# Opening of a fused Nyström attention and MoE kernel: p0 behind the values, identity products in waits, decode ahead of sums

## The chip, the core and the metric

The kernel runs on one core of a Trainium2 chip. Time is device time of one execution in microseconds (us), lower is better. The kernel before took 795.48 us, the median of three runs (795.26, 795.48 and 796.25). The core has five engines with their own instruction streams: PE (matrix products), DVE (vector), ACT (scalar functions, copies), POOL (general), and SP, which here only issues transfers to the DMA engines.

## The reference

Eight batches of attention over 576 positions and 8 heads of 64, with 32 landmarks and an iterated inverse, then one gated feed-forward network over all 4608 tokens:

```python
q_lm, k_lm = means of 18 consecutive rows of q, k      # 32 landmarks
A  = sm(q, k_lm); Bm = sm(q_lm, k_lm); C = sm(q_lm, k)  # softmax of scaled products
Z = Bm.T / (norm1(Bm) * norminf(Bm) + 1e-6)
for _ in range(6):
    Z = 2 * Z - Z @ Bm @ Z
x = (A @ Z @ C @ v) laid out as 4608 x 512
xn = x / sqrt(mean(x * x) + 1e-6) * rms_g
g = xn @ w_gate; val = xn @ w_val                       # 512 x 1536 each
out = (g * sigmoid(g) * val) @ w_out                    # 1536 x 512
```

Everything is float32.

## The kernel before

**Stages.** A batch's attention treats two groups of four heads. `sums` (DVE, line 599) makes the landmark sums of q and k. `Front` makes the scores of landmarks against all positions on PE (`sC`, `sA`), their maxima on DVE, and exponentials on ACT (`E`). `turn` transposes `E` on PE (`sE`, `sF`) and ACT copies it out (`ET`, `EL`). `values` multiplies it with v (PE, `pCV`), and ACT or DVE scales that into the right columns of `PV`. `newton_start` works on the small matrices `Bm` (DVE: `BT`, norms, `nden`). `bmm(BT, BT)` is the first product of the inverse (`p0`, shown as `p<-BT`), and `newton_first` scales it into the left columns of `PV` (DVE, line 1023). Then six `newton_step`s alternate a PE product of 8 pieces (`pn`) with a DVE update (line 1040). `newton_weights` makes the products `pW` and from them `W` and `WT`, and `second` makes the attention output in turned form and its RMS scale: products `pO`, squares on ACT, row sums `pss`, DVE transposes `sqT`, product `pms`, a chain of nine small DVE instructions (lines 1112 to 1126), and at the end the operand `an` as a high and a low part (ACT line 1142, DVE line 1146).

**Feed-forward.** Attention's last matrix is not applied to the tokens: `mix_weights` multiplies the gate and value weights of a pair of 128-column blocks with it (`pM`), and splits the result in `Mhi` and `Mlo` (for the first pair the low part is made by subtracting on PE with the matrix `minus`). `mlp` then walks pairs of blocks: products `psg` (gate) and `psv` (value) of 6 instructions each, silu on ACT (line 528), product with the value half on DVE (line 529), split into `h` (lines 533, 534), and after three pairs the output products `pso`. The weights arrive as raw bytes and are decoded by two ACT instructions (lines 194, 196) and one DVE instruction (line 204) for each block. Block f of the gate is called f-gate below, of the values f-value; pair n holds blocks 2n and 2n+1.

**What sets the order.** Products on PE keep the order in which the program writes them. In `opening()`, the attention of batch 0, all instructions of the other engines are pinned in written order too (`own=pin`). Afterwards `Mixer` weaves the attention of batch 1 (`steady`) into the products of chunk 0: the list `at` says behind which product slot of `mlp` each piece goes (54 for softening, 84, 91, ... for the six Newton steps, 126 for `pW`, `n_gv` = 144 is where the output products begin). On DVE and ACT a scheduler orders what the program leaves free.

**Holds and identity products.** `landed(x)` issues a tiny transfer of one number of x to a scratch tensor (`told`). SP issues transfers in order and holds at the `told` until x has landed, so later loads are held back as well. `spare(n)` and `idle(out, n)` issue n products of the identity with itself into an unused corner of PSUM (`psw<-ident`); nothing reads them. Each float32 product shows as two matmuls in the trace.

**Loads.** SP issues q and k of batch 0, v (512 and 64 KB for a group), then raw weight blocks (`fetch`, line 169, 510.5 KB each) and q and k of batch 1 (`load_qk`, line 584, two of 576 KB for a group). q and k of batch 1 reuse the buffers of batch 0, so their issue waits until PE has read those.

Of the kernel before, what the change touches and what calls it, by code (L numbers as in the profile page):

```python
# [20 lines left out]
P = 128  # L21
# [38 lines left out]
def nystrom_moe_kernel(  # L60
# [53 lines left out]
    def mm(*args, **kw):  # L114
        tc.keep_in_program_order(nc.tensor.matmul(*args, **kw))  # L115
# [155 lines left out]
    def until(chunk, n):  # L271
        while mix.at < (chunk, n):
            yield 0.0
# [299 lines left out]
    with tc.tile_pool(name="ap", bufs=1, side="right") as ap, tc.tile_pool(  # L573
# [6 lines left out]
        def load_qk(b, g):  # L580
            t = qp.tile([P, 2, 2, S], F32, name=f"qk{b}{g}", tag="qk", bufs=2)
            loaded[b, g] = [t[:, 0], t[:, 1]]
            for z in range(2):
                nc.sync.dma_start(loaded[b, g][z], (q, k)[z][b, g])
# [157 lines left out]
        def spare(n):  # L742
            idle(pg.tile([P, 512], F32, name="psw", tag="pg")[:, :P], n)

        def turn(b, g, more=0, own=free):
            E = state[b]["E"][g]
            sE = pa.tile([P, 4, P], F32, name="sE", tag="pa")
            for ch in range(4):
                tp(sE[:, ch], E[:, ch * P : (ch + 1) * P], ident)
            room = pa.tile([P, 2, P], F32, name="sF", tag="pa")  # L750
            sF = room[: 2 * M, 0]
            tp(sF, E[:, 4 * P :], ident)
            idle(room[:, 1], more)
            ET = ap.tile([P, 4, P], F32, name="ET", tag="ET", bufs=2)
            EL = ap.tile([2 * M, P], F32, name="EL", tag="EL", bufs=2)
            own(nc.scalar.copy(ET, sE))
            last = own(nc.scalar.copy(EL, sF))
            if (b, g) == (1, 1):
                early.after = last.ins
            state[b]["ET", g] = ET, EL  # L760
# [21 lines left out]
            else:  # L782
                pin(nc.scalar.mul(to, pCV, by))

        told = dram.tile([1, 2], F32, name="told", tag="told")
        told_at = itertools.count()

        def landed(x):
            n = next(told_at)
            nc.sync.dma_start(told[:, n : n + 1], x)  # L790

        def opening():
            b, own = 0, pin
            for g in range(2):
                sums(b, g, None if g else made.ins, own=own)
            one, two = fronts = [Front(b, g, own) for g in range(2)]
            early.fetch()
            landed(loaded[b, 0, "v"][0][:1, 0, 0, :1])
            for _ in range(3):
                early.fetch()  # L800
            load_qk(1, 0)
            landed(early.raws[1, "v"][0][:1, 0, 0, :1].bitcast(F32))
            load_qk(1, 1)
            for _ in range(4, NF1 + RAWS):
                early.fetch()
            for part in fronts:
                part.tops()
            for part in fronts:
                part.exps()
            one.turned()  # L810
            one.totals()
            two.turned(es=(0,))
            two.totals()
            turn(b, 0, 3, own)
            turn(b, 1, 0, own)
            start = newton_start(b, own)
            BT, den = next(start)
            p0 = bmm(BT, BT, M, "p0")
            for g in range(2):
                values(b, g, 1 - g)  # L820
                load_v(1, g)
            for _ in range(2):
                early.fetch()
            newton_first(b, p0, den, own)
            two.turned(es=(1,))
            lower(b, 0, own=own)
            newton_step(b, 0, own)
            spare(2)
            lower(b, 1, own=own)
            newton_step(b, 1, own)  # L830
            spare(2)
            ends = [early.begin(own) for _ in range(2)]
            expose(b, 0, own)
            expose(b, 1, own)
            ends.extend(early.begin(own) for _ in range(2))
            sums(1, 0, zs=(0,), own=own)
            newton_step(b, 2, own)
            spare(2)
            next(start, None)
            shares(b, 0, own)  # L840
            newton_step(b, 3, own)
            spare(2)
            shares(b, 1, own)
            newton_step(b, 4, own)
            spare(2)
            back(b, 0, own)
            newton_step(b, 5, own)
            spare(2)
            back(b, 1, own)
            newton_weights(b, own)  # L850
            spare(1)
            parts = second(b, own)
            next(parts)
            sums(1, 0, zs=(1,), own=own)
            next(parts)
            ends.extend(early.begin(own) for _ in range(2))
            for _ in range(4):
                ends.pop(0)()
            nxt = Front(1, 0, own)
            load_qk(2, 0)  # L860
            nxt.tops()
            nxt.exps()
            next(parts)
            nxt.turned(es=(0,))
            next(parts)
            low_parts = mix_weights(early, 0, 0, True, own)
            low_parts()
            for _ in parts:
                pass
            nxt.turned(es=(1,))  # L870
            nxt.totals()
            for end in ends:
                end()
            sums(1, 1, own=own)
            early.after = fixed["hi", 0].ins
            for name in ("front", "first", "newton", "wt", "second"):
                stage[name] = 0

# [58 lines left out]
        def steady():  # L937
# [3 lines left out]
            yield from until(0, 12)  # L941
            turn(1, 0)
            yield 0.65, 0.0
            yield from until(0, 46)
            front(1, 1)
            load_qk(2, 1)
# [1 line left out]
            start = newton_start(1)  # L948
            inverse = next(start)
            next(start, None)  # L950
            at = [54, 66, 78] + [84 + 7 * n for n in range(6)] + [126, 136, n_gv + 4, n_gv + 10, n_gv + 18]
            yield from rest(1, inverse, [(0, n) for n in at])
            for b in range(2, B):
                c = b - 2
# [124 lines left out]
        def second(b, own=free):  # L1079
# [17 lines left out]
            sqT = ap.tile([P, NB, M], F32, name="sqT", tag="sqT", bufs=1)  # L1097
            pool, tag = other
            for e in range(2):
                pss = pool.tile([P, 512], F32, name="pss", tag=tag)[:, :HS]  # L1100
                for kk in range(NK):
                    mm(pss[rows(kk), :], ones, sqs[e][:, kk], start=True, stop=True)
                own(
                    nc.vector.transpose(
                        sqT[:, e * (NB // 2) : (e + 1) * (NB // 2), :].rearrange("p n m -> p (n m)"), pss
                    )
                )
            yield 1.1, SQW
            pms = pool.tile([P, 512], F32, name="pms", tag=tag)[:, :NB]
            mm(pms, sel.rearrange("p g t -> p (g t)"), sqT[:, :, 0], start=True, stop=True)  # L1110
            ms = sm.tile([P, NB], F32, name="ms", tag="ms")
            own(nc.vector.tensor_scalar(ms, pms, 1.0 / DM, 1e-6, op0=ALU.mult, op1=ALU.add))
# [12 lines left out]
            own(nc.vector.scalar_tensor_tensor(r2, r2, -10.0 / 3.0, r2, op0=ALU.add, op1=ALU.mult))  # L1125
            own(nc.vector.scalar_tensor_tensor(r1, r2, 5.0, r1, op0=ALU.add, op1=ALU.mult))
            if not b:
                yield
            early_silu = None if b else sm.tile([P, 1], F32, name="tabled", tag="tabled", bufs=1)
            an = mp.tile([P, 2, 2, S], F32R, name="an", tag="an", bufs=2)  # L1130
            rT = ap.tile([P, S], F32, name="rT", tag="sqT", bufs=1)
# [112 lines left out]
        mix.add(steady())  # L1244
        mix.part()
        early.then = fixed["an", 0].ins
        mix.add(early.stream(WAIT))

        def keep(t, ps, ob):
            ob = mp.tile([P, DM], F32, name="ob", tag="ob", bufs=2)  # L1250
# [138 lines left out]
```

## Time and profile before

| | us |
|---|---|
| median of three runs | 795.48 |
| the profiled execution | 794.86 |
| its span, first to last instruction | 793.1 |
| PE busy | 766.6 (97% of the span) |
| DVE busy | 570.0 (72%) |
| ACT busy | 419.8 (53%) |
| POOL busy | 184.2 (23%) |

The page gives busy time by engine for the whole span. PE is busy nine tenths or more in all but the first four of the page's 40 slices (six, seven, eight and seven tenths), which are the first 79 us. How to read a row of a timeline: start and length in us, engine, line of the kernel, operation, what is written and read, the count, and in brackets how long the engine stood idle before it and whose work ended that wait ("issue": nothing that the profile shows). PEclk, the granted clock, is a share of full speed; 1.0 is 2.4 GHz and 0.5 is 1.2 GHz.

### The profile page before, as it was taken

To read this page: it belongs to the slowest core of one execution; us is meant where nothing else is said; L and a number is where in the kernel's file an instruction comes from. 1 tells how busy PE (TensorE), PEld (TensorE's weight loads), DVE (VectorE), ACT (ScalarE), POOL (GpSimd) and SP (SyncE) were. 2 spreads that over 40 slices of the span, in tenths; PEclk is the share of its full clock that TensorE was granted. 3 is DMA by queue.
4 is the path that set the end of the run, shared out by engine and by line. 5 is a ranking of instruction groups with operands and counts; after the bars stand their busy time and mean duration, and the time that the engine had idled before them with its cause. 6 is when DMAs were issued, how large, how long until landed. Compare 5 with 4: busy or idle time off the path is not lost.

```text
span 793.1 us, 17864 instructions
## 1 busy us (share of the span) xinstructions
PE 766.6 (97%) x7002; PEld 618.2 (78%) x7002; DVE 570.0 (72%) x1329; ACT 419.8 (53%) x929; POOL 184.2 (23%) x191
## 2 busy tenths in 40 slices
PE   6787999999999999999999999999999999999998
PEld 5565767778777778778778879897979797979796
DVE  6789897857969858778577574768486757766672
ACT  3588465544545445464475785555355444535450
POOL 0205220110110200200200004353335423433430
PEclk9989999999999999999999999999999999999999
DMA  9957462441552641531556441323332424141412
GB/s 323 336 187 245 125 225 72 166 142 46 186 184 71 187 154 49 186 106 45 174 167 210 159 140 47 132 93 144 94 139 73 158 81 153 59 177 62 171 41 80
DMA packets 55208, 110.83 MB, mean 140 GB/s; under 512 B 5460, under 2 KB 29012, under 8 KB 55124
## 3 DMA queue, kind: packets, MB, share of 16 engines
q1 hardware_dynamic: 55124, 109.69, 41.1%
q8 instruction: 55, 0.90, 0.5%
q14 instruction: 29, 0.24, 0.1%
HBM read 73.69 MB, written 35.98 MB: 138 GB/s over the span
## 4 chain that ended last, share of the span: by engine, by line
PE 89%; DVE 4%; ACT 3%; DMA 2%; issue 1%; POOL 0%; SPq 0%; ACTq 0%; DVEq 0%; POOLq 0%
PE pso L115 38%; PE p L115 17%; PE psg L115 9%; PE psv L115 9%; PE pM L115 5%; PE pn L115 3%; PE sC L115 2%; PE pCV L115 2%; PE pO L115 1%; DMA qk<-in_k_dram 1%; PE pW L115 1%; PE pss L115 1%; PE sE L128 1%; DMA vt<-in_v_dram 1%; DVE lmT L599 1%
## 5 line engine op out<-in xcount | busy, mean ns | idle before, releaser
L115 PE MATMUL pso<-wo,h 128*128 128x512 f32 x648 | 158.4, 396 | 0.0
L115 PEld LDWEIGHTS pso<-wo,h 128*128 128x128 f32 x648 | 118.6, 188 | 31.4 <-ACT E L659 4.2
L115 PE MATMUL pso<-lhio,h 128*128 128x512 f32 x432 | 139.3, 392 | 0.0
L115 PEld LDWEIGHTS pso<-lhio,h 128*128 128x128 f32 x432 | 81.1, 188 | 23.0 <-issue 5.9
L115 PE MATMUL p<-xb,Bwgv 128*128 128x288 f32 x560 | 90.8, 296 | 0.0
L115 PE MATMUL psg<-an,Mhi 128*128 128x288 f32 x384 | 85.7, 307 | 1.8 <-ACT an L1142 1.0
L115 PE MATMUL pso<-lloo,h 128*128 128x512 f32 x216 | 84.4, 391 | 0.0
L115 PE MATMUL psv<-an,Mhi 128*128 128x288 f32 x384 | 83.5, 301 | 0.0
L115 PEld LDWEIGHTS p<-xb,Bwgv 128*128 128x128 f32 x560 | 81.3, 188 | 1.2
L435 POOL TENSOR_TENSOR s<-s,vv 128x576 f32<-128x576 f32 x40 | 57.3, 1434 | 98.6 <-DVE vv L477 96.9
L115 PEld LDWEIGHTS psg<-an,Mhi 128*128 128x128 f32 x384 | 62.3, 191 | 14.3 <-DVE WT L1058 5.0
L115 PE MATMUL p<-xb,Bwo 128*128 128x288 f32 x392 | 70.1, 295 | 0.0
L115 PEld LDWEIGHTS psv<-an,Mhi 128*128 128x128 f32 x384 | 62.3, 189 | 2.1
L1251 ACT COPY ob<-pso 128x512 f32<-128x512 f32 x36 | 21.1, 588 | 74.9 <-PE pso L115 47.3
L115 PEld LDWEIGHTS p<-xb,Bwo 128*128 128x128 f32 x392 | 58.9, 188 | 1.2
L709 POOL TENSOR_TENSOR tA<-tA,mA 128x576 f32<-128x576 f32 x16 | 18.7, 1189 | 176.1 <-DVE mA L708 176.1
L115 PE MATMUL psv<-an,Mlo 128*128 128x288 f32 x192 | 58.8, 306 | 0.0
L115 PE MATMUL psg<-an,Mlo 128*128 128x288 f32 x192 | 58.6, 305 | 0.0
L528 ACT ACTIVATE s<-psg 128x288 f32<-128x288 f32 x96 | 39.3, 409 | 35.2 <-PE psg L115 35.0
L1313 DVE TENSOR_TENSOR obl<-obl,pso 128x512 f32<-128x512 f32 x36 | 24.7, 685 | 43.7 <-PE pso L115 43.0
L529 DVE TENSOR_TENSOR s<-s,psv 128x288 f32<-128x288 f32 x96 | 42.4, 445 | 10.8 <-PE psv L115 8.3
L533 ACT CAST h<-s 128x576 fp32r<-128x576 f32 x48 | 32.2, 671 | 27.9 <-DVE s L529 27.9
(189 smaller groups left out, 1481.5 us busy)
## 6 DMA issues: line engine op xcount, KB each, us to landing
xb<-ad SPq DMA_DIRECT2D x16, 1008.0 KB, 5.4
qk<-in_q_dram SPq DMA_DIRECT2D x16, 576.0 KB, 4.8
qk<-in_k_dram SPq DMA_DIRECT2D x16, 576.0 KB, 6.1
pd<-ob SPq DMA_DIRECT2D x36, 256.0 KB, 3.4
ad<-t SPq DMA_DIRECT2D x64, 144.0 KB, 1.9
obl<-pd SPq DMA_DIRECT2D x36, 256.0 KB, 2.7
out_dram<-obl SPq DMA_DIRECT2D x36, 256.0 KB, 2.0
vt<-in_v_dram SPq DMA_DIRECT2D x16, 512.0 KB, 5.4
```

Of the source, the lines that this page charges most:

```text
L115: tc.keep_in_program_order(nc.tensor.matmul(*args, **kw))
L128: tc.keep_in_program_order(nc.tensor.transpose(*args))
L435: kept(eng.tensor_mul(ss[f][:, e], ss[f][:, e], vv[f][:, e]))
L528: silu["last"] = nc.scalar.activation(s[:, cols], banks[0], AF.Silu).ins
L529: nc.vector.tensor_mul(s[:, cols], s[:, cols], banks[1])
L533: nc.scalar.copy(h[:, 0, TAIL:], s)
L599: nc.vector.tensor_reduce(lms[b, g][:, z], loaded[b, g][z].rearrange("p h (m c) -> p h m c", c=LM), axis=AX.X, op=ALU.add,)
L709: own(nc.gpsimd.tensor_sub(tA, tA, mA.unsqueeze(2).broadcast_to([P, NB, M])))
L1251: nc.scalar.copy(ob, ps)
L1313: kept(nc.vector.tensor_add(ob, ob, ps))
```

## The change

Six edits. The tiny transfers `told` go, with what waited for them, so SP's loads follow each other without these two holds. `p0` is written behind the values of both groups. Six `spare(2)` become `wide()`, one product of the identity with 384 columns. `idle(room, 4)` is added at three places of batch 0: behind the `pss` products, behind the first `pM` and behind the `minus` products. At the end of the opening, where the landmark sums of batch 1, group 1 stood, one block of weights is decoded; the sums and the stream of further decodes are started in `steady`, behind slot 13 of the first chunk. And the numbers of `at` move batch 1's pieces to later slots.

```diff
+        def wide():
+            mm(
+                pg.tile([P, 512], F32, name="psw", tag="pg")[:, : 3 * P],
+                ident,
+                state[0]["ET", 1][0].rearrange("p c t -> p (c t)")[:, : 3 * P],
+                start=True,
+                stop=True,
+            )
...
-        def landed(x):
-            n = next(told_at)
-            nc.sync.dma_start(told[:, n : n + 1], x)
...
             one, two = fronts = [Front(b, g, own) for g in range(2)]
-            early.fetch()
-            landed(loaded[b, 0, "v"][0][:1, 0, 0, :1])
-            for _ in range(3):
+            for _ in range(4):
                 early.fetch()
-            load_qk(1, 0)
-            landed(early.raws[1, "v"][0][:1, 0, 0, :1].bitcast(F32))
-            load_qk(1, 1)
+            for g in range(2):
+                load_qk(1, g)
...
-            p0 = bmm(BT, BT, M, "p0")
             for g in range(2):
                 values(b, g, 1 - g)
                 load_v(1, g)
+            p0 = bmm(BT, BT, M, "p0")
...
             newton_step(b, 0, own)
-            spare(2)
+            wide()
...
-            next(parts)
+            room = next(parts)
             low_parts = mix_weights(early, 0, 0, True, own)
+            idle(room, 4)
             low_parts()
+            idle(room, 4)
...
-            sums(1, 1, own=own)
             early.after = fixed["hi", 0].ins
+            early.load_next()
...
             turn(1, 0)
             yield 0.65, 0.0
+            yield from until(0, 13)
+            early.after = silu["last"]
+            early.load_next()
+            early.after = None
+            sums(1, 1, early.last)
+            mix.add(early.stream(WAIT))
             yield from until(0, 46)
...
-            at = [54, 66, 78] + [84 + 7 * n for n in range(6)] + [126, 136, n_gv + 4, n_gv + 10, n_gv + 18]
+            at = [54, 66, 80] + [88 + 8 * n for n in range(6)] + [136, 142, n_gv + 6, n_gv + 12, n_gv + 20]
...
+            if not b:
+                idle(room[:, 512 - P :], 4)
             yield 1.1, SQW
...
-        mix.add(early.stream(WAIT))
```

On PE, in the opening, between the transposes of `E` and the first Newton steps, the order was as follows (`p` is `p0`, `vt` and `vl` are v, `psw` are identity products):

```order
L128 MATMUL sF<-ident,E 64x128
L115 MATMUL p_339<-BT 32x32 x8
L115 MATMUL pCV<-vt_154,ET 32x64 x16
L115 MATMUL pCV<-vl_155,EL 32x64 x4
L115 MATMUL pCV<-ident 128x128
L115 MATMUL pCV<-vt_158,ET 32x64 x16
L115 MATMUL pCV<-vl_159,EL 32x64 x4
L115 MATMUL pn<-PV 32x96 x8
L115 MATMUL psw<-ident 128x128 x2
```

The same piece now:

```order
L128 MATMUL sF<-ident,E 64x128
L115 MATMUL pCV<-vt_153,ET 32x64 x16
L115 MATMUL pCV<-vl_154,EL 32x64 x4
L115 MATMUL pCV<-ident 128x128
L115 MATMUL pCV<-vt_157,ET 32x64 x16
L115 MATMUL pCV<-vl_158,EL 32x64 x4
L115 MATMUL p_389<-BT 32x32 x8
L115 MATMUL pn<-PV 32x96 x8
L115 MATMUL psw<-ET,ident 128x384
```

The eight pieces of `p0` have moved from ahead of the values to directly ahead of the first `pn`; the count of instructions ahead of `pn` is the same.

On SP, from the first raw weight block on, the issues were (the number behind `qk` tells its buffer: 249 is group 0 of batch 1, 253 is group 1):

```order
L169 DMA wrawg_240<-in_moe_w_gate_dram 128x4x1021
L790 DMA told<-vt_154 1x1
L169 DMA wrawv_243<-in_moe_w_val_dram 128x4x1021
L169 DMA wrawg_245<-in_moe_w_gate_dram 128x4x1021
L169 DMA wrawv_247<-in_moe_w_val_dram 128x4x1021
L584 DMA qk_249<-in_q_dram 128x1152
L584 DMA qk_249<-in_k_dram 128x1152
L790 DMA told<-wrawv_247 1x1
L584 DMA qk_253<-in_q_dram 128x1152
L584 DMA qk_253<-in_k_dram 128x1152
L169 DMA wrawg_256<-in_moe_w_gate_dram 128x4x1021
```

And now (247 is group 0 of batch 1, 250 is group 1):

```order
L169 DMA wrawg_239<-in_moe_w_gate_dram 128x4x1021
L169 DMA wrawv_241<-in_moe_w_val_dram 128x4x1021
L169 DMA wrawg_243<-in_moe_w_gate_dram 128x4x1021
L169 DMA wrawv_245<-in_moe_w_val_dram 128x4x1021
L584 DMA qk_247<-in_q_dram 128x1152
L584 DMA qk_247<-in_k_dram 128x1152
L584 DMA qk_250<-in_q_dram 128x1152
L584 DMA qk_250<-in_k_dram 128x1152
L169 DMA wrawg_253<-in_moe_w_gate_dram 128x4x1021
```

Only the two `told` are gone; the order of the loads is the same, and `qk` still waits for PE's last read of the buffer it goes into.

On DVE, at the start of chunk 0, from the last instruction of batch 1's group 0 (`Bm`) on, with `wgv_578` the weights of pair 1, `wgv_764` those of pair 2 and `lmT` the landmark sums:

```order
L681 TENSOR_SCALAR Bm<-eb,rs 128x32
L204 SCALAR_TENSOR_TENSOR wgv_578<-wrawg_256,wgv_578 128x4x128
L204 SCALAR_TENSOR_TENSOR wgv_578<-wrawv_258,wgv_578 128x4x128
L599 TENSOR_REDUCE lmT<-qk_253 128x64 x2
L204 SCALAR_TENSOR_TENSOR wgv_578<-wrawg_260,wgv_578 128x4x128
L529 TENSOR_TENSOR s<-s,psv 128x288
L204 SCALAR_TENSOR_TENSOR wgv_578<-wrawv_262,wgv_578 128x4x128
L529 TENSOR_TENSOR s<-s,psv 128x288
L204 SCALAR_TENSOR_TENSOR wgv_764<-wrawg_264,wgv_764 128x4x128
```

The same piece now, with `wgv_569` for pair 1 and `wgv_746` for pair 2:

```order
L681 TENSOR_SCALAR Bm<-eb,rs 128x32
L204 SCALAR_TENSOR_TENSOR wgv_569<-wrawg_253,wgv_569 128x4x128
L204 SCALAR_TENSOR_TENSOR wgv_569<-wrawv_255,wgv_569 128x4x128
L204 SCALAR_TENSOR_TENSOR wgv_569<-wrawg_257,wgv_569 128x4x128
L529 TENSOR_TENSOR s<-s,psv 128x288
L204 SCALAR_TENSOR_TENSOR wgv_569<-wrawv_259,wgv_569 128x4x128
L599 TENSOR_REDUCE lmT<-qk_250 128x64 x2
L204 SCALAR_TENSOR_TENSOR wgv_746<-wrawg_261,wgv_746 128x4x128
```

All four blocks of pair 1 now stand ahead of the two sums, and pair 2 behind them.

## Rows read from the trace of the kernel before

**Rows 1.** PE by stretch: us, busy (count), granted clock, DMA share.

```profile
46.00:105.00 59.00, 50.31 (x606) 0.96 0.57 192
105.00:793.00 688.00, 683.48 (x5934) 1.00 0.37 124
```

**Rows 2.** timeline of PE around the first Newton step: start, length, instruction, idle before.

```profile
16.00 0.33 PE L115 MATMUL p<-BT 32*32 32x32 f32 x16 [1.05 <-DVE nsum L992]
...
18.40 0.35 PE L115 MATMUL pn<-PV 32*32 32x96 f32 x2
22.23 0.53 PE L115 MATMUL pn<-PV 32*32 32x96 f32 x14 [3.48 <-issue]
```

**Rows 3.** timeline of DVE in the same stretch.

```profile
17.80 0.23 DVE L1023 TENSOR_TENSOR PV<-p,nden 128x64 f32<-128x64 f32 x1
```

**Rows 4.** timeline of SP, the queue that issues the loads.

```profile
11.20 0.31 SPq L790 DMA_DIRECT2D told<-vt  x1
...
13.62 0.46 SPq L584 DMA_DIRECT2D qk<-in_k_dram  x1
19.35 0.25 SPq L790 DMA_DIRECT2D told<-wrawv  x1
...
24.56 2.72 SPq L169 DMA_DIRECT2D wrawg<-in_moe_w_gate_dram  x1
```

**Rows 5.** DMA of the stretch 0 to 19.6 us: packets and bytes moved.

```profile
DMA packets 3823, 6.30 MB, mean 321 GB/s; under 512 B 734, under 2 KB 2910, under 8 KB 3823
```

**Rows 6.** DMA queues of 19.6 to 19.8 us.

```profile
q8 instruction: 1, 0.02, 33.7%
```

**Rows 7.** DMA queues of 26 to 26.2 us.

```profile
q8 instruction: 1, 0.02, 29.2%
```

**Rows 8.** DMA issues of 14.5 to 29 us: count, size, median to landing.

```profile
wrawg<-in_moe_w_gate_dram SPq DMA_DIRECT2D x3, 510.5 KB, 9.4
...
qk<-in_q_dram SPq DMA_DIRECT2D x1, 576.0 KB, 4.3
```

**Rows 9.** PE in three stretches of lower granted clock.

```profile
23.00:26.50 3.50, 3.50 (x41) 0.53 0.92 293
40.00:47.00 7.00, 5.27 (x20) 0.52 0.56 210
70.80:74.30 3.50, 3.50 (x39) 0.54 0.55 163
```

**Rows 10.** timeline of PE around the first mixed weights.

```profile
30.56 0.71 PE L115 MATMUL psw<-ident 128*128 128x128 f32 x4
...
38.58 0.40 PE L115 MATMUL pms<-sqT,sel 128*128 128x18 f32 x2 [1.78 <-DVE sqT L1104]
...
40.73 1.28 PE L115 MATMUL pM<-Mhi,minus 128*128 128x512 f32 x2 [0.73 <-ACT Mhi L303]
43.02 1.10 PE L115 MATMUL psg<-an,Mhi 128*128 128x288 f32 x2 [1.01 <-ACT an L1142]
```

**Rows 11.** waits of PE from 46 to 106 us: total, times, longest.

```profile
PE pn L115 <- DVE PV L1023: 3.2, 1, 3.2
PE pM L115 <- DVE wgv L204: 1.8, 1, 1.8
```

**Rows 12.** timeline of DVE from 46 us.

```profile
48.17 2.61 DVE L599 TENSOR_REDUCE lmT<-qk 128x64 f32<-128x1152 f32 x2
...
51.66 0.69 DVE L204 SCALAR_TENSOR_TENSOR wgv<-wrawv,wgv 128x512 uint32<-128x512 uint32 x1
...
67.98 1.66 DVE L204 SCALAR_TENSOR_TENSOR w<-wrawo,w 128x512 uint32<-128x512 uint32 x1
...
84.40 0.28 DVE L1054 COPY W<-pW 128x128 f32<-128x128 f32 x1
```

**Rows 13.** timeline of ACT, the decode that the waiting product needs.

```profile
49.52 0.66 ACT L196 ACTIVATE wgv<-wrawv 128x512 int32<-128x512 f32 x1
```

**Rows 14.** DVE from 52 to 88 us: us, busy (count), granted clock, DMA.

```profile
52.00:88.00 36.00, 34.81 (x76) 0.95 0.64 213
```

More of the change, by code (lines that the diff above doesn't have):

```diff
@@ L783, in values @@
                 pin(nc.scalar.mul(to, pCV, by))
-        told = dram.tile([1, 2], F32, name="told", tag="told")
-        told_at = itertools.count()
-        def landed(x):
-            n = next(told_at)
-            nc.sync.dma_start(told[:, n : n + 1], x)
         def opening():
@@ L827, in opening @@
             newton_step(b, 0, own)
-            spare(2)
+            wide()
             lower(b, 1, own=own)
             newton_step(b, 1, own)
-            spare(2)
+            wide()
             ends = [early.begin(own) for _ in range(2)]
@@ L837, in opening @@
             newton_step(b, 2, own)
-            spare(2)
+            wide()
             next(start, None)
@@ L841, in opening @@
             newton_step(b, 3, own)
-            spare(2)
+            wide()
             shares(b, 1, own)
             newton_step(b, 4, own)
-            spare(2)
+            wide()
             back(b, 0, own)
             newton_step(b, 5, own)
-            spare(2)
+            wide()
             back(b, 1, own)
@@ L1099, in second @@
             for e in range(2):
-                pss = pool.tile([P, 512], F32, name="pss", tag=tag)[:, :HS]
+                room = pool.tile([P, 512], F32, name="pss", tag=tag)
+                pss = room[:, :HS]
                 for kk in range(NK):
@@ L1107, in second @@
                 )
+            if not b:
+                idle(room[:, 512 - P :], 4)
             yield 1.1, SQW
-            pms = pool.tile([P, 512], F32, name="pms", tag=tag)[:, :NB]
+            room = pool.tile([P, 512], F32, name="pms", tag=tag)
+            pms = room[:, :NB]
             mm(pms, sel.rearrange("p g t -> p (g t)"), sqT[:, :, 0], start=True, stop=True)
@@ L1127, in second @@
             if not b:
-                yield
+                yield room[:, P : 2 * P]
             early_silu = None if b else sm.tile([P, 1], F32, name="tabled", tag="tabled", bufs=1)
```

## The prediction

> **What bounds the kernel now.** I read PE by stretches first. From 105 us to the end PE works 683.5 of 688.0 us at full clock; from 46 to 105 it works 50.3 of 59.0 [rows 1]. The change leaves the work behind 105 us as it is, so the time moves by as much as PE reaches that point sooner or later. A gain can come from two places only: the opening up to 46 us, and the idle and slow time between 46 and 105.
>
> Next I read PE's timeline in the opening. The reader is to see one row with 3.48 us of idle time ahead of it and "issue" as the releaser: the first Newton step sends one of its eight products at 18.40 and the other seven at 22.23 [rows 2]. No data was missing. The DMA views name a candidate: the first 16 KB packet of the instruction queue moves at 19.6 to 19.8 us [rows 6], and PE goes on 2.4 us behind it. I take the stall to be a late fetch of PE's instructions. Until 19.6 us 6.30 MB had moved [rows 5], and SP had issued its last big load at 13.62 [rows 4]. With the sizes in the rows (six of q and k at 576 KB, four raw blocks at 510.5 KB [rows 8], 1.2 MB of v) that is 6.8 MB issued. So the fetch ran when nearly all that SP had issued was through.
>
> A third view is the waits of PE between 46 and 105 us: 3.2 us for `PV` of line 1023 and 1.8 us for a weight decode of pair 1 [rows 11]. The last view is PE's clock: three stretches of 3.5, 7.0 and 3.5 us at about half, the lower of the two levels [rows 9].
>
> **The change part by part.**
>
> *p0 behind the values.* It removes no instruction. PE idled 1.05 us ahead of `p0` [rows 2], time in which the values of group 0 can now run. The step that follows cannot begin much sooner all the same: it needs the scaled `p0`, which DVE made at 17.80, when `nden` was ready [rows 3]. So `pn` can come at about 18.1 in place of 18.4, 0.3 us. Behind it lies the stall, which ends when the fetch ends and not when PE arrives: 0.
>
> *The two told go.* SP issued nothing between its first raw block and 11.20 and between 13.62 and 19.35 [rows 4]. Now three raw blocks, and q and k of group 1, are issued sooner. They bring no bytes ahead: the DMA moved 6.30 MB in 19.6 us, at a mean of 321 GB/s [rows 5], and a queue that is never empty is drained no faster for being longer. What is issued ahead of the fetch decides. Up to q and k of group 0 the list is the same in both kernels; q and k of group 1 wait for PE's last read of their buffer in either. If the fetch stands behind the same 6.3 MB, it runs at 19.6 us again. Value taken: 0. From below: the stall goes, minus 3.5. From above: the fetch stands behind the 2 x 576 KB = 1.18 MB of group 1 as well, at the mean rate of 0.321 MB/us [rows 5] plus 3.7.
>
> *wide.* Six times one product of 384 columns in place of two of 128: and four PE instructions fewer each time. A pair took 0.71 us at full clock [rows 10], beside DVE's update of `PV`. PE waits for that update in most steps, so whatever it is worth is hidden: 0, or 0.3 us either way if a wide one outlasts the update.
>
> *Three times idle(4).* Two identity products took 0.71 us [rows 10], so four take an estimated 1.4. The waits they go into are 1.78 (ahead of `pms`), 0.73 (ahead of the minus products) and 1.01 (ahead of the first `psg`) [rows 10]. The first fits. The second overruns by 0.7 and the third by 0.4: up to plus 1.1, if the clock is as before. Against this stands the clock: from 40 to 47 us it was about half [rows 9], right behind the stretch with those three waits. From 43.02 to 47 the products `psg` and `psv` ran at that rate; at full clock these 4 us of work would be 2. So minus 2.0 if the clock holds, and plus 1.1 if not. I take minus 0.5, nearer the gain, but discounted: behind it PE waits for the decode of pair 1 anyway, and that moves only as far as `an` and ACT move.
>
> *Decode ahead of the sums.* PE waited 1.8 us for the second half of pair 1 [rows 11]. Its DVE instruction ran at 51.66, behind two sums of 2.61 us together that began at 48.17 [rows 12]; ACT's part of the same block was done at 49.52 + 0.66 = 50.18 [rows 13]. With the sums behind it the DVE part can run at 50.2 to 50.9, so `pM` comes 1.55 us sooner. The 2.61 us are not gone: they now lie ahead of the decodes of pair 2 and of batch 1's chain. From 52 to 88 us DVE works 34.81 of 36.0 us [rows 14], so it can give little of that back later, and the gain at `pM` is not the gain at 105. Bounds: minus 1.55 and, if all 2.61 us come back in front of a product that waits, plus 1.1.
>
> *Later slots for batch 1.* The first of batch 1's Newton steps comes four slots later, and they stand eight slots apart in place of seven, so the 3.2 us wait for `PV` of line 1023 [rows 11] shrinks: DVE ran one decode of 1.66 us right ahead of it [rows 12], which now stands behind. What remains is limited by DVE, which is full. Against it, `W` is copied later in DVE's order. For these two edits together I take minus 0.8, the middle between minus 2.7 (the 1.55, and 1.2 idle us of DVE in that stretch) and plus 1.1.
>
> The sum: 0 + 0 + 0 - 0.5 - 0.8 = -1.3. The profiled execution took 794.86, its span of 793.1 and 1.76 around it; 794.86 - 1.3 = 793.56. The median of the runs lies 0.62 above that execution, so 794.2.
>
> What is left out above is the Trainium skill's word on the stall. Its page "Runtime: NRT & Kernel Launch", section "Instruction fetch mechanics", says that an engine fetches its next block of instructions while it works on the current one, and that this is mostly hidden. The trace does not agree: 3.48 us are not hidden here. By the page the stall would be no term at all.
>
> **The rivals.**
>
> *The fetch is served sooner.* For it: a second packet of the instruction queue moved at 26.0 to 26.2 us [rows 7], while SP was held for 2.72 us at a full queue [rows 4] and loads took 9.4 us from issue to landing [rows 8]. So a fetch does pass loads that were issued. If the first one does that with the fuller queue, `pn` runs on from 18.1 in place of 22.23, less what DVE, POOL and the landing weights hold back: I take 3.0 of the 4.1 us. 794.2 - 3.0 = 791.2. Against it: the first fetch had to wait in an equally full queue before. The Trainium skill, "DMA: Bandwidth & Descriptors", section "Queues, rings and completion order", states this rival's rule: each DMA engine takes turns between its queues, packet by packet. The first stall of this trace speaks against it, the second packet for it.
>
> *The fetch stands behind more.* The holds kept SP's backlog short: a load issued at 19.70, behind the second hold, landed 4.3 us later in place of 9.4 [rows 8]. Without them q and k of group 1 are issued behind PE's read of that buffer, some 6 us sooner. If the fetch is asked for behind that point, it waits for 1.18 MB more: plus 3.7 us, 794.2 + 3.7 = 797.9, slower than before. It decides from the moment that the request comes later than the issue of group 1's q. Against it: those 3.7 us show only if PE has nothing behind to catch up with, and the second fetch was not held by the whole backlog.
>
> *W takes the place of the wait.* `pW` moves ten slots and `pO` six, so four slots less lie between. A copy of `W` ran at 84.40 [rows 12] with no wait of PE. If a 1.3 us sum (half of 2.61 [rows 12]) stands ahead of it, `pO` waits for about that: 794.2 + 1.3 = 795.5, no difference that can be measured; with both sums ahead it would be 796.8.
>
> **How the numbers follow.** What a measurement of this kernel can tell from no change is about 0.2%, 1.6 us: below 793.9 is faster, above 797.1 slower. The forecast, the stall as it is and some gain behind it, has a chance of 0.43; its own range is 792.5 to 796.2, of which 0.18 lies below 793.9, 0.24 within and 0.01 above. The sooner fetch has 0.25, all of it faster. The later fetch has 0.22, 0.18 slower and 0.04 within. The late `W` has 0.10, 0.06 within and 0.04 slower. Faster 0.43, same 0.34, slower 0.23. The range takes the sooner fetch's 791.2 with its 0.6 us below and the later fetch's 797.9 with 0.5 above: 790.6 to 798.4.
>
> **What would show it.** PE's row with "issue" ahead of the seven products of the first Newton step, and the time of the first packet of the instruction queue: 22.2 and 19.6 us if I am right, earlier than 19 or later than 22 if one of the rivals is. The granted clock from 40 to 47 us: near 1.0 if the identity products hold it. PE's wait for the second half of pair 1 should be under 0.5 us in place of 1.8, and its wait for `PV` of line 1023 under 2 us. If PE has idle time ahead of `pO` of batch 1, `W` is the new wait. The forecast is wrong if the stall moves by over 1 us either way.

## The result and the profile after

The changed kernel took 799.50 us (median of four runs, 799.0 to 800.59) against 795.87 for the kernel before beside it (four runs, 795.26 to 796.37): ratio 1.0051, 95% interval 1.0038 to 1.0063. It is slower, and lies above the forecast range of 790.6 to 798.4. Its profiled execution took 799.47, with a span of 797.7 us, 4.6 more than before.

Three stages share these 4.6 us. The first `psg` comes at 42.53 in place of 43.02 [rows 10], 0.5 us sooner. From there to the scores of batch 2's group 1 it takes 62.7 us (42.53 to 105.24) in place of 58.75 (43.02 to 101.77), 4.0 more. From there to the end it is 1.1 us longer.

The stretch from 46 us on, PE by windows (us, busy with count, granted clock, DMA share and GB/s). The first row is the kernel before up to these scores ([rows 1] run 3.2 us past them), the other two are the changed kernel:

```profile
46.00:101.80 55.80, 47.73 (x564) 0.96 0.55 184
...
46.00:105.20 59.20, 49.45 (x551) 0.94 0.52 169
105.00:112.00 7.00, 6.14 (x52) 0.76 0.76 267
```

Idle time is 59.20 - 49.45 = 9.75 us here, against 55.80 - 47.73 = 8.07, and it is in other places. From the first `psg` to the scores PE is idle for 1.8 us more and busy for 2.1 us more (52.8 in place of 50.7) with the same products. The clock doesn't explain the second part, since its mean over this stretch is 0.95 here and was 0.94; 1.2 us of it are in `pM` (5.1 in place of 3.9). Up to the scores of batch 1's group 1 little is lost yet (12.2 us from the first `psg`, 12.0 before), so nearly all of the 4.0 us lies behind them. The last row is new: right behind batch 2's scores the clock falls again, some 3.4 us at half, which is enough for the 1.1 us.

The opening on PE, which answers to [rows 2]:

```profile
14.52 0.65 PE L115 MATMUL pCV<-vt,ET 128*32 128x64 f32 x32 [0.20 <-ACT ET L765]
...
16.60 0.33 PE L115 MATMUL p<-BT 32*32 32x32 f32 x16
17.55 0.24 PE L115 MATMUL pn<-PV 32*32 32x96 f32 x1 [0.63 <-DVE PV L1030]
20.52 0.53 PE L115 MATMUL pn<-PV 32*32 32x96 f32 x15 [2.74 <-issue]
```

The values begin at 14.52, before `p0`. The stall at the first Newton step is still there, but it is 2.74 us in place of 3.48 and ends 1.7 us sooner. The first packet of the instruction queue moves sooner too (queue of 17.8 to 18.0 us; before: [rows 6]):

```profile
q8 instruction: 1, 0.02, 33.0%
```

Next the stretch that answers to [rows 10], with the identity products (`pss<-ident`, `pms<-ident`) that the change adds:

```profile
37.41 1.16 PE L115 MATMUL pss<-ident 128*128 128x128 f32 x8 [1.76 <-DVE sqT L1112]
38.41 0.29 PE L115 MATMUL pms<-sqT,sel 128*128 128x18 f32 x2
...
39.65 1.16 PE L115 MATMUL pms<-ident 128*128 128x128 f32 x8
40.57 0.87 PE L115 MATMUL pM<-Mhi,minus 128*128 128x512 f32 x2
41.27 1.05 PE L115 MATMUL pms<-ident 128*128 128x128 f32 x8
42.53 0.89 PE L115 MATMUL psg<-an,Mhi 128*128 128x288 f32 x2 [0.21 <-ACT an L1153]
```

The reader is to see the first row: the four products meant for the wait behind `pss` stand *behind* it. They are the ones that wait 1.76 us for `sqT`, and `pms` follows them 1.0 us later. Their corner lies in the bank of `pss`, and that bank is free only when DVE has read it. The second four run while ACT makes `Mhi`, the third four ahead of `psg`.

The clock, which answers to [rows 9]: from 40 to 47 us it is full now, and lower from 72 to 79 us, twice as long as the 3.5 us of before.

```profile
40.00:47.00 7.00, 6.67 (x47) 1.00 0.51 186
72.00:74.00 2.00, 1.11 (x4) 0.58 0.31 125
74.00:76.00 2.00, 2.00 (x21) 0.50 0.58 96
76.00:78.00 2.00, 2.00 (x23) 0.50 0.42 168
78.00:80.00 2.00, 2.00 (x24) 0.71 0.00 0
```

What PE waits for from 46 to 108 us (total, times, longest), which answers to [rows 11]:

```profile
PE psg L115 <- ACT s L528: 3.8, 2, 3.6
PE psg L115 <- DVE s L529: 1.4, 1, 1.4
```

The two waits of before are gone: `pM` of pair 1 does not wait for its weights, and the first `pn` not for line 1023's `PV`. In their place stand waits for the silu (`s` of line 528) and for DVE's product behind it. The longest stands behind `pM` of pair 2:

```profile
67.08 2.22 PE L115 MATMUL pM<-wgv,WT 64*32 64x512 f32 x16 [1.02 <-ACT s L528]
72.89 0.85 PE L115 MATMUL psg<-an,Mhi 128*128 128x288 f32 x2 [3.59 <-ACT s L528]
```

ACT around it:

```profile
69.46 0.62 ACT L216 CAST wo<-w 128x512 fp32r<-128x512 f32 x1
71.88 0.67 ACT L196 ACTIVATE w<-wrawo 128x512 int32<-128x512 f32 x1 [1.80 <-POOL wo L217]
72.45 0.39 ACT L528 ACTIVATE s<-psg 128x288 f32<-128x288 f32 x1
72.74 1.06 ACT L303 CAST Mhi<-pM 128x512 fp32r<-128x512 f32 x2
```

The silu and the two copies `Mhi` stand behind the decode of the third block of w_out, and this one waits 1.80 us for POOL. The decoded block goes into one of two buffers, and the first is free when POOL has subtracted its low part (line 217). POOL did that late, behind two other jobs:

```profile
66.43 2.27 POOL L726 TENSOR_TENSOR tA<-tA,rA 128x576 f32<-128x576 f32 x2 [3.23 <-DVE sumA L723]
68.65 1.86 POOL L1026 COPY blocks<-Bs 32x64 f32<-32x64 f32 x4
70.58 1.26 POOL L217 TENSOR_TENSOR wo<-w,wo 128x512 fp32r<-128x512 f32 x1
```

The same decode holds DVE as well (row 2 below, 1.75 us), with the product of silu and `psv` (line 529) behind it. Row 1 shows the two sums in their new place. The `psg` that waits 1.4 us for DVE, until 53.08, waits for a product of line 529 behind these sums: the 1.8 us that `pM` of pair 1 no longer waits come back here, and in a wait of 0.6 us ahead of a `psv`.

```profile
49.45 2.61 DVE L599 TENSOR_REDUCE lmT<-qk 128x64 f32<-128x1152 f32 x2
...
72.58 1.28 DVE L204 SCALAR_TENSOR_TENSOR w<-wrawo,w 128x512 uint32<-128x512 uint32 x1 [1.75 <-ACT w L196]
```

### The profile page after: what moved, and what is told of

Read it like the earlier page. It is cut to its first block, busy times and chain, and to the rows that moved or that the text cites. A ratio compares the mean times of both kernels' runs of the same rounds, so it can differ in the third digit from the quotient of the medians.

```text
span 797.7 us, 17884 instructions
## 1 busy us (share of the span) xinstructions
PE 773.6 (97%) x7014; PEld 619.9 (78%) x7014; DVE 568.3 (71%) x1329; ACT 420.6 (53%) x929; POOL 182.7 (23%) x191
## 4 chain that ended last, share of the span: by engine, by line
PE 87%; DVE 6%; ACT 3%; issue 2%; DMA 1%; POOL 0%; SPq 0%; ACTq 0%; DVEq 0%; POOLq 0%
PE pso L115 38%; PE p L115 17%; PE psg L115 9%; PE psv L115 8%; PE pM L115 5%; PE pn L115 2%; PE sC L115 2%; PE pCV L115 1%; DVE lmT L599 1%; PE pO L115 1%; PE pss L115 1%; PE pW L115 1%; DMA qk<-in_k_dram 1%; PE sE L128 1%; DVE wgv L204 1%
## 5 line engine op out<-in xcount | busy, mean ns | idle before, releaser
L115 PEld LDWEIGHTS psg<-an,Mhi 128*128 128x128 f32 x384 | 62.4, 191 | 18.3 <-DVE WT L1065 5.0
L709 POOL TENSOR_TENSOR tA<-tA,mA 128x576 f32<-128x576 f32 x16 | 18.3, 1162 | 177.0 <-DVE mA L708 177.0
L529 DVE TENSOR_TENSOR s<-s,psv 128x288 f32<-128x288 f32 x96 | 42.5, 447 | 13.5 <-PE psv L115 8.7
```

The costliest lines, as they stand in the source:

```text
L529: nc.vector.tensor_mul(s[:, cols], s[:, cols], banks[1])
L709: own(nc.gpsimd.tensor_sub(tA, tA, mA.unsqueeze(2).broadcast_to([P, NB, M])))
```

## The experiments

All times stand beside runs of the kernel before on the same chip; ratios are to it, with 95% intervals.

**The opening alone, and each half of the later part.** The first kernel is the changed one with sums, stream and slots as before:

```diff
-            early.load_next()
+            sums(1, 1, own=own)
...
-            at = [54, 66, 80] + [88 + 8 * n for n in range(6)] + [136, 142, n_gv + 6, n_gv + 12, n_gv + 20]
+            at = [54, 66, 78] + [84 + 7 * n for n in range(6)] + [126, 136, n_gv + 4, n_gv + 10, n_gv + 18]
```

> The changed kernel with the landmark sums, the decode stream and the list of slots as before: only the opening's edits are left (no holds, p0 behind the values, wide products, idle products). Theory: the opening is 1.9 us ahead at the end of its fourth pair of psg and psv groups and the loss lies behind it, so this is faster than before, about 794 us (1.9 gained, some of it lost at DVE). Rival, that the holds or the identity products cost the time: 797 or more.

Measured: 796.0 (794.42 to 798.41), ratio 1.0008 (0.9996 to 1.0020). No gain, so my theory of an opening worth 1.9 us fell. The next two put back only the slots, or only the sums and the stream.

> The changed kernel with the old list of slots. In ACT's order the decode of the third w_out block, which waits for POOL, then stands behind the silu and not ahead of it. Theory (that decode holds the silu, and with it PE): most of the 3.6 us wait of psg goes, 795.5 to 797. Rival 1, the later slots cost everything by themselves: 794. Rival 2, the moved sums cost everything: 799.5.

> The changed kernel with sums and decode stream as before and the new slots. The third decode of w_out again stands behind silu and Mhi. Theory: 794.5 to 796.5, since both edits together bring the decode ahead of the silu. Rival 1, the later slots cost everything: 799.5. Rival 2, the moved sums cost everything: 794.

Measured: 796.85, ratio 1.0022 (1.0010 to 1.0034), with the old slots; 797.08, ratio 1.0015 (1.0005 to 1.0024), with the old sums. The second is a little more than expected. Putting either back takes over half of the loss away. Against the opening alone (1.0008) the moved sums and stream cost 1.1 us, the slots 0.6 and both together 3.4. The traces can't confirm these sizes: from the first `psg` to batch 2's scores both kernels take 60.0 us (45.45 to 105.45; 45.05 to 105.06), against 58.55 for the opening alone and 62.7 for both edits, but in these two executions the clock had fallen ahead of the first `psg`, which came some 2.5 us later than in the other two.

**POOL out of the way of the third decode.** The changed kernel, where DVE makes the first low part:

```diff
-                    self.low.tensor_sub(lo, wf, hi.bitcast(F32))
+                    (nc.vector if f == 0 else self.low).tensor_sub(lo, wf, hi.bitcast(F32))
```

> The changed kernel, but the low part of the first w_out block is made by DVE (an estimated 0.7 us more there) and not by POOL, so that the buffer of the third decode comes free without POOL's queue; the order on ACT at that place stays. Theory: ACT's 1.8 us wait and PE's 3.6 us wait for the silu shrink by 1.5 or more, and the time to 796.5 to 798. If the order alone or something else is the cause: 799.5.

Measured: 797.6, ratio 1.0032 (1.0017 to 1.0048), as the theory said. PE's wait for that silu, and ACT's third decode, which no longer waits for POOL:

```profile
69.66 3.10 PE L115 MATMUL pM<-wgv,WT 64*32 64x512 f32 x16 [1.01 <-ACT s L528]
74.04 0.85 PE L115 MATMUL psg<-an,Mhi 128*128 128x288 f32 x2 [1.29 <-ACT s L528]
```

```profile
73.03 0.66 ACT L196 ACTIVATE w<-wrawo 128x512 int32<-128x512 f32 x1
```

The wait fell from 3.59 to 1.29 us, in part because `pM` ahead of it ran longer at half clock (3.10 in place of 2.22). From the start of that `pM` to the `psg` it takes 4.38 us in place of 5.81, 1.4 less. By the ratios (1.0051 and 1.0032) the wait for POOL is 1.5 of the 4.1 us; their intervals overlap, so the size is uncertain.

**The holds alone.** The kernel before without the two `told`:

```diff
-            landed(loaded[b, 0, "v"][0][:1, 0, 0, :1])
...
-            landed(early.raws[1, "v"][0][:1, 0, 0, :1].bitcast(F32))
```

> The kernel before, without the two told transfers and nothing else. Theory: their removal alone brings the first fetch packet forward, from 19.7 to about 18.2 us, and the first Newton step goes on at about 20.8 in place of 22.2; the time 794.3 to 795.0 against 795.6. Rival: the holds have nothing to do with it and p0's place brought the stall forward; then 22.2 again and 795.6.

Measured: 795.56, ratio 1.0003 (0.9994 to 1.0012). The stall is the one of before to the hundredth:

```profile
15.73 0.33 PE L115 MATMUL p<-BT 32*32 32x32 f32 x16 [1.04 <-DVE nsum L990]
...
21.96 0.85 PE L115 MATMUL pn<-PV 32*32 32x96 f32 x14 [3.48 <-issue]
```

The expected shift did not come; the rival was right: the holds have nothing to do with it.

**p0 alone.** The kernel before with one move:

```diff
-            p0 = bmm(BT, BT, M, "p0")
             for g in range(2):
                 values(b, g, 1 - g)
                 load_v(1, g)
+            p0 = bmm(BT, BT, M, "p0")
```

> The kernel before with p0 behind the values of both groups and nothing else. Theory: the first fetch packet moves 3.4 us after PE's first product of the values, wherever that stands (16.32 and 19.7 before; 14.5 to 15.1 and 17.9 to 18.3 in the kernels with p0 moved), so it comes 1.2 to 1.4 us sooner and the stall ends at 20.8 to 21.0; the time is 1 us less than before, 794.3 to 794.9. Rival: the stall keeps its end at 22.2 and the time is that of before.

Measured: 794.28 (793.07 to 795.37), ratio 0.9983 (0.9974 to 0.9991). This is faster, by 1.35 us, and the lowest ratio of all kernels here. PE, and the instruction queue of 17.9 to 18.2 us:

```profile
14.67 0.65 PE L115 MATMUL pCV<-vt,ET 128*32 128x64 f32 x32 [0.19 <-ACT ET L756]
...
20.66 0.86 PE L115 MATMUL pn<-PV 32*32 32x96 f32 x15 [2.73 <-issue]
```

```profile
q8 instruction: 1, 0.02, 23.0%
```

The stall's end moved as expected. That this is what gives the 1.35 us isn't shown by this trace: it is of the slowest of the twelve executions (795.37), PE's clock was 0.50 from 20 to 28 us (0.86 and 0.72 in the two halves before), and the first `psg` came at 43.08, no sooner than the 43.02 of before.

**When is the fetch asked for?** The kernel before, with the first hold waiting for `ET`, so that the DMA engines run empty. The loads are written behind the transposes and stay in the same order.

```diff
-            landed(loaded[b, 0, "v"][0][:1, 0, 0, :1])
+            held = landed(state[b]["ET", 0][0][:1, 0, :1])
+            with tc.issue_after(held.ins):
...
```

> The kernel before, with the first hold on SP waiting for ET (ready at about 15.1 us) and not for v, so that the DMA engines have nothing to do from about 13 to 16 us. If the fetch stands behind the bytes that SP has issued, its packet moves by 16 us and there is no stall at the first Newton step. If it is asked for only as PE comes to the values, it moves at 18 us or later and the stall stays at 2 us or more. The time itself rises, since the weights land later.

Measured, one execution: 796.34. PE's window of 14 to 16 us (share 0.02 and 5 GB/s of the DMA), the instruction queue of 18.2 to 18.4 us, and the stall:

```profile
14.00:16.00 2.00, 0.96 (x25) 1.00 0.02 5
```

```profile
q8 instruction: 1, 0.02, 39.0%
```

```profile
20.79 0.86 PE L115 MATMUL pn<-PV 32*32 32x96 f32 x14 [2.38 <-issue]
```

With nothing to move, no fetch moved either; it came at 18.3 us, 2.3 us behind the first product of the values (15.98 in this run), in place of 3.4 us with loaded engines. The bytes that SP has issued are not what it stands behind. The request itself is in no trace. That it comes when PE reaches about that place is inferred from the packet, which keeps its distance to the first product of the values in every kernel here. I put the part of the load at about 1.1 us (3.4 - 2.3), an estimate from this one execution, in which the engines were three quarters busy again from 16 to 18 us.

**The identity products.** First the opening's edits without the four behind `pss`, then with these in a bank of their own, then with pairs in place of the wide products. The edit of the second:

```diff
-                idle(room[:, 512 - P :], 4)
+                spare(4)
```

> The opening's edits alone (old sums, old slots) without the first of the three idle(4), the one behind the pss products. Theory: those products stand in a bank that DVE still reads, so they run behind the wait for sqT and hold pms for 1.0 us; without them pms follows sqT at once, psg comes 1.0 us sooner and the time is 1.0 us less than with them (796.0), about 795.0. Rival: they keep the clock up and their lack costs what they hold: 796 or more, with the clock of 40 to 47 us lower.

> The opening's edits alone, with the first idle(4) written to a bank of its own in place of the corner of the pss bank. Theory: now they run in the wait for sqT and hold nothing, so pms comes 1.0 us sooner and the clock stays as with them: 794.5 to 795.0. Rival: four products of 0.29 us at full clock last longer than the wait at half clock and the time stays at 796.

> The opening's edits alone, with two products of 128 columns again in place of one of 384 behind each Newton step. Theory: at half clock a wide product (1.54 to 1.65 us) outlasts DVE's update, a pair (1.1 to 1.22) hardly does, so two or three steps behind the stall get 0.4 us shorter: 795.0 to 795.5 against 796.0. Rival: the wide ones keep the clock up in the steps and without them more of the opening is at half clock: 796.5 or more.

Measured: without them 794.78, ratio 0.9999 (0.9987 to 1.0011); own bank 794.36, ratio 0.9992 (0.9983 to 1.0001); pairs 796.23, ratio 1.0008 (0.9995 to 1.0021), as with the wide ones (1.0008, 0.9996 to 1.0020). The first two came as the theory said, though their intervals overlap with that of the opening alone; of the pairs neither the gain nor the loss came. Whether the first four products hold the clock up is open: from 40 to 47 us it was 0.88 without them and 1.00 with them in their own bank, in one execution each. In the bank of their own they run in the wait:

```profile
36.84 1.16 PE L115 MATMUL psw<-ident 128*128 128x128 f32 x8
38.69 0.40 PE L115 MATMUL pms<-sqT,sel 128*128 128x18 f32 x2 [0.70 <-DVE sqT L1106]
```

`pms` follows DVE at once, and from the end of the wait for `sqT` to the first `psg` it takes 4.2 us (38.69 to 42.92) in place of 5.1 (37.58 to 42.70 in the opening alone). So the 1.0 us on the path is shown. Between wide products and pairs no difference can be measured.

The last question was what the twelve products give on top of p0's place. Two kernels: p0 alone with the three `idle(4)` as the change places them, and with the first in its own bank.

> The kernel before with p0 behind the values (1.35 us faster by itself) and the three idle(4) as the change places them. Theory: the first of them holds pms for 1.0 us, the others give back a part by the clock; so 0.5 to 1.5 us slower than with p0 alone, ratio to before 0.9990 to 1.0005. Rival, that they hold the clock up and pay: ratio 0.9983 or less.

> The same with the first idle(4) in a bank of its own, so that it runs in the wait for sqT. Theory: about 1.0 us less than with it behind the wait, ratio to before 0.9975 to 0.9985, the best of all kernels here. Rival, that identity products there are worth nothing: the ratio of p0 alone, 0.9983, or more.

Measured: 796.14, ratio 1.0014 (1.0002 to 1.0026), and 794.61, ratio 0.9991 (0.9981 to 1.0000). Both expectations were too kind: against p0 alone (0.9983) the products cost 2.5 us as placed, more than I allowed, and in the better place they still give nothing. The trace of the first is of one of its two slowest executions (799.10) and shows what happens when the clock falls:

```profile
37.80 1.16 PE L115 MATMUL pss<-ident 128*128 128x128 f32 x8 [1.76 <-DVE sqT L1107]
38.79 0.29 PE L115 MATMUL pms<-sqT,sel 128*128 128x18 f32 x2
39.02 1.57 PE L115 MATMUL pM<-wgv,WT 64*32 64x512 f32 x16
40.52 2.08 PE L115 MATMUL pms<-ident 128*128 128x128 f32 x8
...
44.51 0.89 PE L115 MATMUL psg<-an,Mhi 128*128 128x288 f32 x2 [0.37 <-ACT an L1148]
```

In this execution the clock fell at about 39.5 us all the same. Then the second four took 2.08 us (1.16 at full clock) and stand ahead of the minus products, and `psg` came 6.7 us behind the end of the wait for `sqT` in place of 5.1 in the changed kernel's profile. Where the clock held, the gain went into a wait, as in the second kernel:

```profile
42.11 0.89 PE L115 MATMUL psg<-an,Mhi 128*128 128x288 f32 x2 [0.20 <-ACT an L1147]
...
51.58 1.53 PE L115 MATMUL pM<-wgv,WT 64*32 64x512 f32 x16 [2.94 <-DVE wgv L204]
```

`psg` was 0.9 us sooner than before, the products behind it ran at full clock, and PE then waited 2.94 us for pair 1's weights in place of 1.75. At batch 2's scores nearly nothing of the full clock was left: 58.55 us from the first `psg` to there, against 58.75.

**The later part alone.** The kernel before with the sums and the stream moved, and the kernel before with the new slots; each edit is that of the change:

```diff
-            sums(1, 1, own=own)
+            early.load_next()
...
+            yield from until(0, 13)
+            early.after = silu["last"]
+            early.load_next()
+            early.after = None
+            sums(1, 1, early.last)
+            mix.add(early.stream(WAIT))
```

> The kernel before with the sums of batch 1's group 1 and the decode stream moved as in the change, and nothing else. Theory: from the first psg to the scores of batch 2's group 1 it takes 60.0 us (as with the new opening) in place of 58.75, so 796.5 to 797. Rival, that the move costs only together with the new opening: 795.5 or less, as the pM of pair 1 comes 1.5 us sooner.

> The kernel before with the new list of slots and nothing else. Theory: the same 60.0 us in place of 58.75, since pM of pair 2 now stands ahead of the Newton steps and takes banks that wait for a silu; 796.5 to 797. Rival, that the later slots give PE the 3.15 us wait for the first pn back: 794.

Measured: 798.11, ratio 1.0040 (1.0027 to 1.0053), more than expected, and 796.69, ratio 1.0018 (1.0007 to 1.0029). Each loses by itself. With the sums moved, ACT waits for POOL as in the changed kernel, and PE waits behind it:

```profile
74.59 0.67 ACT L196 ACTIVATE w<-wrawo 128x512 int32<-128x512 f32 x1 [1.55 <-POOL wo L217]
75.16 1.05 ACT L303 CAST Mhi<-pM 128x512 fp32r<-128x512 f32 x2
```

```profile
76.75 0.40 PE L115 MATMUL psv<-an,Mhi 128*128 128x288 f32 x1 [1.76 <-DVE s L529]
```

With the new slots, `pM` of pair 2 stands ahead of the first Newton step and waits for a silu to free its bank, and the `psg` behind it again:

```profile
66.86 2.47 PE L115 MATMUL pM<-wgv,WT 64*32 64x512 f32 x16 [0.59 <-ACT s L528]
71.08 0.85 PE L115 MATMUL psg<-an,Mhi 128*128 128x288 f32 x2 [1.75 <-ACT s L528]
```

Last, the moved sums with the first low part made by DVE (the edit of the POOL experiment):

> The kernel before with sums and decode stream moved (ratio 1.0040), and the low part of the first w_out block made by DVE and not by POOL. Theory: most of the loss is the third decode's wait for POOL with silu, Mhi and DVE's products queued behind it; then 1 to 2.5 us less, ratio 1.001 to 1.0025. Rival, that the sums' own place costs the time: 1.0035 or more.

Measured: 795.89, ratio 1.0007 (0.9997 to 1.0016). ACT's third decode follows at once:

```profile
72.18 0.68 ACT L196 ACTIVATE w<-wrawo 128x512 int32<-128x512 f32 x1
```

By the ratios this takes 2.6 of the 3.2 us away, and the intervals lie apart, so here the wait for POOL is shown as the cause of most of the loss. The two traces show less of it: from the first `psg` to batch 2's scores 59.9 us in place of 61.1, while their first `psg` differs by 1.4 us (42.73 and 44.12) ahead of any difference between the two programs. How much the sums' own place costs is open: the ratios leave 0.6 us for it, while in both traces it takes 13.3 to 13.5 us from the first `psg` to the scores of batch 1's group 1, in place of 12.0.

## Why the prediction was wrong

- **What bounds.** Right but for the 1.1 us right behind batch 2's scores: from 112 to 400 us PE works 287.8 and 287.9 of 288.0 us at full clock in both kernels.
- ***p0 behind the values*: the step failed, in the other direction.** I let the stall end at a fixed time and swallow the 0.3 us. In fact the stall's end moves with PE's arrival at the values: it came at 20.5 to 21.2 us in the eleven kernels with p0 moved and at 21.7 to 22.2 in the five without (the late hold left out), 1.2 us sooner on average. The whole time became 1.35 us less; that the one makes the other fits in size, but no trace follows it to the end.
- ***The two told go*: 0, and 0 was measured** (1.0003). Both rivals about the fetch were wrong as mechanisms. The fetch came sooner, at 17.9 us, which the prediction had named as the sign of the sooner fetch, but by p0's place and not by the holds. The later fetch would have given 797.9, near the measured 799.5, but by chance: no run shows a fetch held by more bytes. What the Trainium skill says in "Runtime: NRT & Kernel Launch", "Instruction fetch mechanics", that the next block is fetched while the current one is worked on, can't be read from these traces, which have no request; that the packet keeps its distance to a place that PE passes ahead of the stall speaks for it. "Mostly hidden" is not borne out at this first fetch, with a stall of 2.4 to 3.75 us in every trace here.
- ***wide*: 0, as said.** At half clock one takes 1.54 us and outlasts DVE's update, but between the two kernels no difference can be measured.
- ***Three times idle(4)*: minus 0.5 was wrong in sign.** "The first fits" failed: it could not run in the wait, because its bank was what the wait was about. It cost 1.0 us on the path to `psg`. (Four took 1.16 us at full clock, not the estimated 1.4, so it wasn't their length.) The upper bound for the other two (plus 1.1) was near what the trace shows when the clock falls: 5.7 us from `pms` to `psg` (38.79 to 44.51) in place of 4.4 (38.58 to 43.02). The gain when it holds ended in the wait for pair 1, as the prediction feared.
- ***Decode ahead of the sums* and *Later slots*: minus 0.8 was the main failure.** Behind the same opening the two cost 3.4 us (1.0051 against 1.0008), against a bound of plus 1.1. The two named waits did go: `pM` of pair 1 waited no more, and the 3.2 us for the first `pn` went. But the 1.8 us at `pM` came back as waits for DVE's product behind the sums, so up to the scores of batch 1's group 1 nothing was gained (12.2 us from the first `psg` in place of 12.0). (The 1.55 us hoped for at `pM` were also a little high: the rows give 51.66 - 50.2 = 1.46.) And the step priced DVE's work and put at nothing that the stream of decodes moves with it. An earlier third decode of w_out stands ahead of `Mhi` on ACT, and with the later slots ahead of a silu as well, and waits there for POOL. The sums and the stream by themselves cost 3.2 us, most of it this wait; the slots by themselves cost 1.4 us without it, by their trace through `pM` of pair 2 ahead of the first Newton step and the silu that it and the next `psg` wait for. In the profile before, the same wait for POOL was there, but behind the silu of 70.80; what queued behind it was not asked:

```profile
72.33 0.70 ACT L196 ACTIVATE w<-wrawo 128x512 int32<-128x512 f32 x1 [0.56 <-POOL wo L217]
```

- **The rival *W takes the place of the wait*:** `pW` waited 0.2 us for DVE, `pO` not at all. Not so.

The parts by themselves (told 0.2, p0 -1.35, identity products +2.5, sums and stream +3.2, slots +1.4 us, each a ratio times 795.4) come to 6.0 against 4.1 measured. Each has an interval of about 1 us either way, so this doesn't show whether they add up. The opening as a whole cost 0.6 with either pair or wide products, which can't be told from nothing. How the sums and the slots share the loss when both are there is open: 3.2 and 1.4 us with the old opening, 1.1 and 0.6 with the new one, and 3.4 for both.

## What to carry to other kernels

A filler put into a wait runs there only if its own output is free: write it to a bank that the wait is not about, and expect a cost whenever the clock falls. Before work is pulled forward on an in-order engine, read what the moved instruction itself waits for, and what will queue behind it. And a stall with no data missing may be a fetch that follows the engine's progress: here, reaching the place sooner by reordering waits moved the stall's end. Last, a kept trace is one execution: before its stretches are compared with those of another, see where its time lies among the runs and whether the clock ahead of the stretch was the same.

## What the runs showed of the hardware

- The first 16 KB of instructions moved 2.3 us behind PE's first product of the values where the DMA engines had just been idle (one kernel), and 3.3 to 3.7 us behind it with loaded ones, in the sixteen other kernels, wherever that product stood (14.5 to 16.3 us).
- The granted clock of the same stretch differs between executions of the same code. Up to the first `psg` the opening is word for word the same in the changed kernel and in the first four kernels above; that `psg` came at 42.53, 42.70, 45.45, 45.05 and 45.12 us, with the clock from 40 to 47 us at 1.00, 1.00, 0.76, 0.77 and 0.77. That alone is some 2.5 us, as much as most of the effects here, and why only many runs tell them apart.
